# Seven of eight blocks of the second pass with seven products instead of five of eight

## The chip, the cores and the metric

The kernel runs on one core of a Trainium2 chip. The metric is the device time of one execution in microseconds (us), here the median of several. The core has TensorE (PE, with its weight loads as PEld), VectorE (DVE), ScalarE (ACT), GpSimd (POOL) and SyncE (SP), which here issues nearly all DMAs. Each engine works through its own queue in program order; engines wait for each other by semaphores. SBUF is the on-chip memory, PSUM the accumulators of TensorE.

## The reference

Lightning attention over 4 x 8 heads gives x (4 x 768 x 512). A mixer follows, and then a two-layer network whose hidden layer has 2048 columns. Everything is fp32; the weights arrive as 64-bit numbers.

```python
xt = x.transpose(0, 2, 1)
h = xt @ U @ V                                # rank 32 along the sequence
u = x + h.transpose(0, 2, 1)                  # 3072 rows of 512
ch = np.maximum(u @ w_ch1, 0.0) @ w_ch2       # 512 -> 2048 -> 512
return (u + ch).astype(np.float32)
```

`u @ w_ch1` is the first product, with its result r kept in DRAM until the second product, `max(r, 0) @ w_ch2`, reads it.

## The kernel before, in words

**fp32 by parts.** A product of fp32 numbers is made of three products of rounded parts. Each operand is split into a high part (ScalarE, a multiplication by nearly one), a low part (VectorE, the operand minus its high part) and a third (a combination of the two, on VectorE or POOL). One product over 128 input channels is then three matmuls of 128x512: high by high and low by low into one accumulator, third by third into another, or into the same one after `raise_high` (ScalarE, in place) has scaled it between. The matmuls of the first two parts are called highs below, those of the third part thirds. A `raise_high`, or a drain of PSUM by ScalarE (`taken`) or VectorE (`add_to`, L1190), stands between them.

**The first product** goes over 24 groups of 128 rows, four to a column group g of 512, so g = 0 to 5, and over 16 tiles ft of 128 columns of the hidden layer. Groups 0 to 3 are the first pass. From 144 us on it runs as 56 units, one (g, ft) each of 12 matmuls (`run_unit`, L989): the highs of this unit, then the thirds of the unit two before. In each unit, steps of other work are emitted that have been strewn over units by number (`strew`, L1041): converting the 64-bit words of a tile of w1 or w2 to fp32 (`weight_steps`, L114: a load of 512 KB of words, five VectorE and two ScalarE instructions), splitting it (w1) or keeping it in DRAM (w2), and preparing what the second pass needs. A step that comes at unit n is placed on its engine behind what was emitted before.

**The second pass** does groups g0 = 4 and g1 = 5 in eight blocks j, each of two column tiles ft = 2j and 2j + 1. Input channels are halved too, so a block is a 2 x 2 by 2 x 2 product of quarters: a11, a12 (u of g0, lower and upper channels), a21, a22 (g1) and the four quarters of the weights. A block in `eight_of` (L1262) makes the plain eight products, 48 matmuls. A block in `seven_of` (L1205) uses Winograd's form with seven products of sums and differences, 42 matmuls. The forms of u are a11, a12, s1 = a21 + a22, s2 = s1 - a11, s4 = a12 - s2, s3 = a11 - a21, a22, and a21 for plain blocks. Those of the weights are the four quarters and four differences, made by VectorE (`form_steps`, L1009, four instructions a block) and kept in DRAM (`forms_d`). The results of a seven are assembled from PSUM by VectorE's `add_to` and stored with `give`; an eight drains with ScalarE alone.

The order of products in a seven is (0, a11), (4, s1), the seventh product (7, a22) of the block before, (1, a12), (5, s2), (3, s4), (6, s3). `SEVEN` (L944) names the blocks with seven products: 0, 2, 3, 5 and 6. In the code z, d, p5, p3 and c11 are the accumulators of a seven; `pz` are those of a plain block.

**The stream.** The weight forms come back in the order of use (`sequence`), two to a tile, through `divided_steps` (L255): a load of two times 128 KB by SP into one of three wf buffers, a high on ScalarE (L276), a low on VectorE (L279) and a third on POOL (L285). Each product in the second pass calls `tick` once after its highs, which emits what is strewn at that step (or tick). Tile t, used from step 2t on, is loaded at step 2t - 8, gets its high at 2t - 4 and its low and third at 2t - 3 (L1151). Its splits go to a rotation of five tiles. Steps also hold the last four w2 conversions (`W2_LATE`, L946), the splits of the first four tiles of w2 (`w2_split`, L1361) and the first fetches and splits of r for the second product (`fetch`, `split`, into rm and m).

**The forms of u** (`form`, L1097) are made in the last ten units and the first steps: a high on ScalarE (L1103), a rest on VectorE (L1106, into s_hl) and a third on VectorE (L1109, into s_d), each over 128x1024. The list `late` holds ScalarE work that is emitted at the start of the next unit or step.

**The second product** goes over g and ft, four 128-row groups each, 1152 matmuls, with ScalarE and VectorE splitting r (L1303 to L1305) three steps ahead.

All orders named are written out by hand and kept on each engine; only behind the second pass a scheduler interleaves the first steps of the second product with the last of the pass.

Of the kernel before, what the change touches and what calls it, by code (L numbers as in the profile page):

```python
# [18 lines left out]
def kernel(  # L19
# [28 lines left out]
    nc = tc.nc  # L48
# [38 lines left out]
    late = []  # L87
# [167 lines left out]
    def divided_steps(parts, fetch, engine, apart=False, raw=None):  # L255

        st = {}

        def load():
            st["w"] = raw() if raw and apart else plain({}, 0)()  # L260
            fetch(st["w"])

        def split():
            hi, low, third = parts()
            w = st["w"][:, 0 : hi.shape[-1]]
            nc.scalar.mul(hi, w, E * NEAR)
            nc.vector.scalar_tensor_tensor(
                low, hi.bitcast(FP32), -1.0 / E, w, ALU.mult, ALU.add
            )
            engine.tensor_tensor(  # L270
                out=third, in0=low.bitcast(FP32), in1=hi.bitcast(FP32), op=ALU.subtract
            )

        def high():
            st["hi"], st["low"], st["third"] = parts()
            nc.scalar.mul(st["hi"], st["w"][:, 0 : st["hi"].shape[-1]], E * NEAR)  # L276

        def low():
            nc.vector.scalar_tensor_tensor(  # L279
                st["low"], st["hi"].bitcast(FP32), -1.0 / E,  # L280
                st["w"][:, 0 : st["hi"].shape[-1]], ALU.mult, ALU.add,
            )

        def third():
            engine.tensor_tensor(  # L285
                out=st["third"], in0=st["low"].bitcast(FP32), in1=st["hi"].bitcast(FP32),
                op=ALU.subtract,
            )

        return [load, high, low, third] if apart else [load, split]  # L290
# [562 lines left out]
    def enter_first_product(s):  # L853
        nonlocal r_pool
        att_ctx.close()
        words_pool[:] = [wconv]
        r_pool = ctx.enter_context(tc.tile_pool(name="r", bufs=8, reuse_waits="tile"))
        set_ends(r_pool.tile([P, P], FP32, tag="ends", bufs=1, name="ends"))
        more_w.append(ctx.enter_context(tc.tile_pool(name="w1_more", bufs=2, reuse_waits="tile")))
        plain_pool.append(  # L860
            ctx.enter_context(tc.tile_pool(name="plain", bufs=2, reuse_waits="tile"))
        )
        whole_pool.append(
            whole_ctx.enter_context(tc.tile_pool(name="whole", bufs=NG - FG, reuse_waits="tile"))
        )
# [62 lines left out]
    for i, (pair, ft) in enumerate(head):  # L928
# [8 lines left out]
    mix_ctx.close()  # L937
    sums_pool = whole_ctx.enter_context(tc.tile_pool(name="sums", bufs=2, reuse_waits="tile"))
    tags.append(("wt", "wf"))
    words_pool += 2 * [  # L940
        mid_ctx.enter_context(tc.tile_pool(name="words", bufs=2, side="right", reuse_waits="tile"))
    ]
    HC = C // 2
    SEVEN = (0, 2, 3, 5, 6)  # L944
    LAST = FT - 4
    W2_LATE = (6, 8, 24, 26)  # L946


    one = iter(range(1 << 30))
# [91 lines left out]
    def strew(units, steps):  # L1041
        assert len(units) == len(steps)
        for n, step in zip(units, steps):
            at.setdefault(n, []).append((units[0], step))
# [9 lines left out]
    strew((4, 4, 5, 5, 5), form_steps(0))  # L1054
    for ft, n in ((4, 3), (5, 7)):
        strew(after(n, FIRST), w1_steps(ft))
    for ft, n in zip(range(6, FT), (10, 14, 18, 22, 26, 28, 32, 33, 35, 37)):
        strew(after(n, W1), w1_steps(ft))
    for n in (5, 9, 12, 16, 20, 24, 30, 39, 42, 45, 48, 51):
        strew(after(n, W2), later.pop(0))  # L1060
    for j, n in ((2, 9), (3, 16), (4, 25), (5, 30), (6, 35), (7, 40)):
        strew((n, n, n + 1, n + 1, n + 1) if j in SEVEN else (n,), form_steps(j))
    units = [(g, ft) for ft in range(2, LAST) for g in range(FG)]
    units += [(g, ft) for g in range(FG) for ft in range(LAST, FT)]
# [12 lines left out]
    for n in range(0, len(sequence), 2):  # L1077

        def parts(n=n):
            stream[n // 2] = t = w_tile(FT + n // 2)  # L1080
            k = HC * len(sequence[n : n + 2])
            return [t[:, i, 0:k] for i in range(3)]

        def fetch(w, n=n):
            for i, (j, form) in enumerate(sequence[n : n + 2]):
                nc.sync.dma_start(out=w[:, i * HC : (i + 1) * HC], in_=forms_d[j][:, form])

        stream_steps.append(divided_steps(parts, fetch, nc.gpsimd, True))

    places, form_of = {}, {}  # L1090

# [5 lines left out]
    def form(key, n, i, of):  # L1097

        hl, d = form_of[key] = places[n][i]
        hi, low = hl[:, 0], hl[:, 1]  # L1100

        def high():
            nc.scalar.mul(hi, of, NEAR)  # L1103

        def rest():
            nc.vector.tensor_tensor(out=low, in0=of, in1=hi.bitcast(FP32), op=ALU.subtract)  # L1106

        def last():
            nc.vector.scalar_tensor_tensor(  # L1109
                d, hi.bitcast(FP32), E, low.bitcast(FP32), ALU.mult, ALU.subtract  # L1110
            )

        return [high, rest, last]
# [16 lines left out]
    for n, (g, ft) in enumerate(units):  # L1130
        if n == 46:
            place(0)
            strew((46, 47, 48), form("a11", 0, 0, a11))
            strew((47, 48, 49), form("a12", 0, 1, a12))
            strew((50,), sums(a12, a12, s2))
        if n == 50:
            place(1)
            strew((50, 51, 52), form("s1", 1, 0, s1))
            strew((51, 52, 53), form("s2", 1, 1, s2))
            strew((53,), sums(s3, a11, a21))  # L1140
        if n == 54:
            place(2)
            strew((54, 55, 55), form("s4", 2, 0, a12))
            a22_steps = form("a22", 2, 1, a22)
            strew((55,), a22_steps[:1])
        run_unit(g, ft, sorted(at.pop(n, ()), key=lambda what: what[0]))
    assert not at
    strew((0, 0), stream_steps[2][2:])
    strew((1, 2, 2), stream_steps[3][1:])
    for t in range(4, len(stream_steps)):  # L1150
        strew((2 * t - 8, 2 * t - 4, 2 * t - 3, 2 * t - 3), stream_steps[t])  # L1151
    strew((0, 0), a22_steps[1:])
    def last_forms():
        place(3)
        s3_steps, a21_steps = form("s3", 3, 0, s3), form("a21", 3, 1, a21)
        strew((1, 2, 2), s3_steps)
        strew((3, 4, 4), a21_steps)
        strew((4,), [forms_made])

    def forms_made():  # L1160
        whole_ctx.close()
# [199 lines left out]
    def w2_split(ft):  # L1361
        def raw():
            t = e_pool[0].tile([P, 3, C], F32R, tag="e", name="w2")
            w2t[ft] = [t[:, i, :] for i in range(3)]
            return w2t[ft][2].bitcast(FP32)

        if ft >= 4 and ft % 4 == 0:
            hl = hl_pool.tile([P, 4, 2, C], F32R, tag="hl", name="w2_hl")
            d = d_pool.tile([P, 4, C], F32R, tag="d", name="w2_d")
            for i in range(4):  # L1370
                w2t[ft + i] = [hl[:, i, 0], hl[:, i, 1], d[:, i]]
        return divided_steps(
            lambda: w2t[ft], lambda w: nc.sync.dma_start(out=w, in_=w2_d[ft]), nc.vector,
            ft < 4, raw,
        )

# [9 lines left out]
    strew((total - 14,), [begin_second])  # L1386
    for ft in range(4):
        strew(
            (total - 13 + 2 * ft, total - 6 + ft, total - 5 + ft, total - 5 + ft), w2_split(ft)
        )  # L1390
    for n in range(3):
        strew((total - 5 + n,), [lambda n=n: fetch(n)])
# [64 lines left out]
```

## Time and profile before

| what | us |
|---|---|
| median of 3 runs | 649.53 (649.27 to 653.06) |
| the profiled execution | 649.79 |
| its span, first to last instruction | 648.0 |
| TensorE busy, share of the span | 636.8, 98% |
| VectorE busy | 449.9, 69% |
| ScalarE busy | 329.7, 51% |
| POOL busy | 141.3, 22% |
| first pass in units (PE) | 142 to 295 |
| second pass in blocks (PE) | 295 to 382 |
| second product (PE) | 382 to 644 |

Most busy times in the profile are of pipelined instructions: a 128x512 matmul is listed with 389 ns, and the next one starts long before it ends. What counts is the distance of starts. In a timeline row stand the start, the time that the row's instructions cover, the engine, the line, the operation, output and inputs, and how many instructions were merged; in brackets the idle time before them and what ended it. DVE rows of 0.68 us that follow each other start 0.60 apart. The granted clock is the share of full speed that TensorE was allowed.

### The profile page before, as it was taken

The numbers are of one execution on the slowest core, as the hardware profiler recorded it, in microseconds if no ns is written. First come the engines' busy times: TensorE is split into PE (matmuls) and PEld (weight loads), VectorE is DVE, ScalarE is ACT, GpSimd is POOL, SyncE is SP. The second block draws the span as 40 slices with busy tenths as digits, with TensorE's granted clock in tenths as the row PEclk, the third lists the DMA queues.
The fourth block names the chain that finished last, engine by engine and source line by source line (L and its number), as shares of the span: only waits on it lengthen the run. The fifth ranks groups of instructions, "written<-read, shape, count | busy, mean of one in ns | idle before, by whom it ended". The sixth has DMA issues, their size and how long they took to land.

```text
span 648.0 us, 13566 instructions
## 1 busy us (share of the span) xinstructions
PE 636.8 (98%) x5212; PEld 534.0 (82%) x5212; DVE 449.9 (69%) x714; ACT 329.7 (51%) x604; POOL 141.3 (22%) x120
## 2 busy tenths in 40 slices
PE   8999999999999999999999999999999999999997
PEld 7989989778888888886878878888888888888886
DVE  5766878567776688589867799785575665755754
ACT  3775766436676777678657574232322322322320
POOL 3575978000000000013343400030030300300300
PEclk9999999999999999999999999999999999999999
DMA  9979985348967787456577798353362353442521
GB/s 227 249 181 277 246 224 159 128 165 295 312 238 272 248 281 258 180 204 228 196 232 240 252 301 281 103 190 134 96 228 98 121 204 99 170 155 97 180 82 65
DMA packets 140227, 127.91 MB, mean 197 GB/s; under 512 B 82370, under 2 KB 97602, under 8 KB 140162
## 3 DMA queue, kind: packets, MB, share of 16 engines
q1 hardware_dynamic: 115040, 120.62, 58.0%
q10 hardware_dynamic: 25122, 6.42, 4.4%
q8 instruction: 41, 0.67, 0.4%
q14 instruction: 24, 0.20, 0.1%
HBM read 77.86 MB, written 48.76 MB: 195 GB/s over the span
## 4 chain that ended last, share of the span: by engine, by line
PE 74%; DVE 1%; issue 1%; DMA 1%; ACT 0%; DVEq 0%; SPq 0%; ACTq 0%
PE pz L957 28%; PE pz L1321 13%; PE pz L1319 13%; PE pd L1323 13%; PE z L957 2%; PE p L957 1%; DMA wf<-forms_d 1%; PE d L957 1%; DVE s_hl L1106 1%; PE c L957 1%; PE pd L900 0%; DVE w L279 0%; PE pz L889 0%; ACT p L964 0%; ACT s_hl L1103 0%
## 5 line engine op out<-in xcount | busy, mean ns | idle before, releaser
L1303 ACT ACTIVATE m<-rm 128x512 fp32r<-128x512 f32 x96 | 60.6, 631 | 168.3 <-PE pd L1323 141.3
L1304 DVE SCALAR_TENSOR_TENSOR m<-rm,m 128x512 fp32r<-128x512 f32 x96 | 71.6, 746 | 84.1 <-ACT m L1303 84.1
L1319 PE MATMUL pz<-w_hl,m 128*128 128x512 f32 x288 | 112.0, 389 | 0.0
L1321 PE MATMUL pz<-w_hl,m 128*128 128x512 f32 x288 | 112.0, 389 | 0.0
L1323 PE MATMUL pd<-w_d,m 128*128 128x512 f32 x288 | 110.7, 389 | 0.0
L957 PE MATMUL pz<-u_hl,w 128*128 128x512 f32 x448 | 110.3, 389 | 0.0
L957 PEld LDWEIGHTS pz<-u_hl,w 128*128 128x128 f32 x448 | 84.1, 188 | 17.4
L285 POOL TENSOR_TENSOR w<-w 128x512 fp32r<-128x512 f32 (+1 forms) x24 | 35.1, 1468 | 227.9 <-DVE w L279 208.3
L1305 DVE SCALAR_TENSOR_TENSOR m<-m 128x512 fp32r<-128x512 f32 x96 | 74.4, 776 | 2.7
L1348 POOL TENSOR_TENSOR o<-o,u 128x512 f32<-128x512 f32 x20 | 29.8, 1518 | 198.5 <-DVE o L1344 198.5
L1319 PEld LDWEIGHTS pz<-w_hl,m 128*128 128x128 f32 x288 | 54.1, 188 | 11.3
L1321 PEld LDWEIGHTS pz<-w_hl,m 128*128 128x128 f32 x288 | 54.1, 188 | 11.2
L1323 PEld LDWEIGHTS pd<-w_d,m 128*128 128x128 f32 x288 | 54.1, 188 | 11.2
L957 PE MATMUL pz<-u_d,w 128*128 128x512 f32 x224 | 59.7, 389 | 0.0
L964 ACT ACTIVATE pz<-pz 128x512 f32<-128x512 f32 x68 | 39.4, 581 | 31.8 <-PE pz L957 31.8
L957 PEld LDWEIGHTS pz<-u_d,w 128*128 128x128 f32 x224 | 42.0, 188 | 8.8
L196 DVE SCALAR_TENSOR_TENSOR sc<-words,sc 128x512 uint32<-128x512 uint32 (+2 forms) x34 | 24.5, 721 | 34.8 <-ACT sc L178 34.8
L968 ACT ACTIVATE r<-pz 128x512 f32<-128x512 f32 x68 | 40.2, 594 | 14.2 <-PE pz L957 13.2
L472 DVE TENSOR_TENSOR sm<-pss,mask 128x512 f32<-128x512 f32 x48 | 30.9, 685 | 19.3 <-PE pss L463 19.3
L1319 PE MATMUL pz<-w,m 128*128 128x512 f32 x96 | 37.4, 390 | 0.0
L1321 PE MATMUL pz<-w,m 128*128 128x512 f32 x96 | 37.4, 389 | 0.0
L1323 PE MATMUL pd<-w,m 128*128 128x512 f32 x96 | 37.3, 390 | 0.0
(143 smaller groups left out, 1081.4 us busy)
## 6 DMA issues: line engine op xcount, KB each, us to landing
r_d<-r SPq DMA_DIRECT2D x96, 256.0 KB, 2.4
rm<-r_d SPq DMA_DIRECT2D x96, 256.0 KB, 2.6
words<-in_moe_w_ch_dram SPq DMA_DIRECT2D x30, 512.0 KB, 4.5
u_d<-x_nat SPq DMA_DIRECT2D x24, 256.0 KB, 4.1
u<-u_d SPq DMA_DIRECT2D x24, 256.0 KB, 4.3
wf<-forms_d SPq DMA_DIRECT2D x47, 128.0 KB, 3.1
qraw<-in_q_dram SPq DMA_DIRECT2D x23, 256.0 KB, 5.1
out_dram<-o SPq DMA_DIRECT2D x23, 256.0 KB, 2.0
```

Source lines behind the costliest of these rows:

```text
L285: engine.tensor_tensor(out=st["third"], in0=st["low"].bitcast(FP32), in1=st["hi"].bitcast(FP32), op=ALU.subtract,)
L472: nc.vector.tensor_tensor(out=sm[:, x], in0=pss[:, x], in1=mask[:, x], op=ALU.mult)
L957: nc.tensor.matmul(out=out, lhsT=weights, rhs=moving, start=start and i == 0, stop=i == len(pieces) - 1, skip_group_check=not start,)
L964: nc.scalar.mul(acc, acc, 1.0 + E)
L968: nc.scalar.mul(r, acc, 4096.0)
L1303: nc.scalar.activation(out=m[:, 0], in_=r, func=AF.Relu, scale=NEAR)
L1304: nc.vector.scalar_tensor_tensor(m[:, 1], r, 0.0, hi, ALU.max, ALU.subtract)
L1305: nc.vector.scalar_tensor_tensor(m[:, 2], hi, E, low, ALU.mult, ALU.subtract)
L1319: nc.tensor.matmul(out=pz, lhsT=m[:, 0, cols], rhs=hi, start=first, stop=False)
L1321: nc.tensor.matmul(out=pz, lhsT=m[:, 1, cols], rhs=low, start=False, stop=end)
L1323: nc.tensor.matmul(out=pd, lhsT=m[:, 2, cols], rhs=third, start=first, stop=end)
L1348: nc.gpsimd.tensor_tensor(out=o, in0=o, in1=u, op=ALU.add)
```

## The change

Blocks 4 and 7 become sevens: `SEVEN` is now 0 and 2 to 7, and only block 1 makes eight products. The stream then has 53 forms in 27 tiles instead of 47 in 24. The rest moves or re-places other work:

- Of u's forms, s4 and s3 are made before the second pass, with their high parts first on ScalarE at unit 54; a22 and a21 are made in its first eight steps. Before, s4 and a22 came first and s3 and a21 in the steps.
- The thirds of the stream's first four tiles are made by VectorE, not POOL; the thirds of w2's first four tiles by POOL, not VectorE.
- Conversions of w1 and w2 in the units come at other units, the last of w2 starting at 46 instead of 51; the four late ones start at steps 7, 9, 16 and 22 instead of 6, 8, 24 and 26.
- The first four w2 splits are spread from 24 to 3 steps ahead of the pass's end instead of 13 to 2.
- The pool of words gets three buffers instead of two (four places with the first one), the pool of r seven instead of eight.

```diff
-        r_pool = ctx.enter_context(tc.tile_pool(name="r", bufs=8, reuse_waits="tile"))
+        r_pool = ctx.enter_context(tc.tile_pool(name="r", bufs=7, reuse_waits="tile"))
...
-    words_pool += 2 * [
-        mid_ctx.enter_context(tc.tile_pool(name="words", bufs=2, side="right", reuse_waits="tile"))
+    words_pool += 3 * [
+        mid_ctx.enter_context(tc.tile_pool(name="words", bufs=3, side="right", reuse_waits="tile"))
     ]
     HC = C // 2
-    SEVEN = (0, 2, 3, 5, 6)
+    SEVEN = (0, 2, 3, 4, 5, 6, 7)
     LAST = FT - 4
-    W2_LATE = (6, 8, 24, 26)
+    W2_LATE = (7, 9, 16, 22)
...
-    for ft, n in zip(range(6, FT), (10, 14, 18, 22, 26, 28, 32, 33, 35, 37)):
+    for ft, n in zip(range(6, FT), (10, 11, 15, 17, 20, 25, 29, 30, 32, 36)):
         strew(after(n, W1), w1_steps(ft))
-    for n in (5, 9, 12, 16, 20, 24, 30, 39, 42, 45, 48, 51):
+    for n in (6, 16, 21, 24, 27, 34, 38, 40, 42, 43, 45, 46):
         strew(after(n, W2), later.pop(0))
-    for j, n in ((2, 9), (3, 16), (4, 25), (5, 30), (6, 35), (7, 40)):
+    for j, n in ((2, 9), (3, 13), (4, 19), (5, 27), (6, 32), (7, 38)):
         strew((n, n, n + 1, n + 1, n + 1) if j in SEVEN else (n,), form_steps(j))
...
-        stream_steps.append(divided_steps(parts, fetch, nc.gpsimd, True))
+        stream_steps.append(
+            divided_steps(parts, fetch, nc.vector if n < 8 else nc.gpsimd, True)
+        )
...
             place(2)
-            strew((54, 55, 55), form("s4", 2, 0, a12))
-            a22_steps = form("a22", 2, 1, a22)
-            strew((55,), a22_steps[:1])
+            s4_steps, s3_steps = form("s4", 2, 0, a12), form("s3", 2, 1, s3)
+            late.extend([s4_steps[0], s3_steps[0]])
+            strew((54, 54), s4_steps[1:])
+            strew((55, 55), s3_steps[1:])
...
-    strew((0, 0), a22_steps[1:])
     def last_forms():
         place(3)
-        s3_steps, a21_steps = form("s3", 3, 0, s3), form("a21", 3, 1, a21)
-        strew((1, 2, 2), s3_steps)
-        strew((3, 4, 4), a21_steps)
-        strew((4,), [forms_made])
+        strew((1, 3, 4), form("a22", 3, 0, a22))
+        strew((5, 6, 8), form("a21", 3, 1, a21))
+        strew((8,), [forms_made])
...
-            lambda: w2t[ft], lambda w: nc.sync.dma_start(out=w, in_=w2_d[ft]), nc.vector,
+            lambda: w2t[ft], lambda w: nc.sync.dma_start(out=w, in_=w2_d[ft]),
+            nc.gpsimd if ft < 4 else nc.vector,
             ft < 4, raw,
...
-            (total - 13 + 2 * ft, total - 6 + ft, total - 5 + ft, total - 5 + ft), w2_split(ft)
+            (total - 24 + 5 * ft, total - 20 + 5 * ft, total - 19 + 5 * ft, total - 18 + 5 * ft),
+            w2_split(ft),
```

## The prediction

> **What bounds the kernel now.** I read the page's table of busy time first, then the groups, then the windows of the seven-product stage, and last the chain and the timeline around each gap.
>
> ```profile
> PE 636.8 (98%) x5212; PEld 534.0 (82%) x5212; DVE 449.9 (69%) x714; ACT 329.7 (51%) x604; POOL 141.3 (22%) x120
> ...
> 144.40 147.80 PE pz L957 x652
> ```
>
> TensorE is the bound, and the second line (the chain in order of time) gives its price: 652 matmuls of 128x512 in 147.80 us, 0.2267 us each, with no gap from 144 to 292 us. From 384 us to the end the second product keeps the same pace. So the change can win in two ways only: fewer matmuls, and fewer gaps between 292 and 384 us, the second pass with blocks. The windows show where these gaps are.
>
> ```profile
> 290.00:300.00 10.00, 10.00 (x45) 8.09 (x44) 8.76 (x7) 8.07 (x15) 4.16 (x3) 1.00 0.63 211
> 300.00:310.00 10.00, 8.39 (x30) 6.17 (x29) 9.86 (x11) 5.47 (x9) 2.82 (x3) 0.83 0.57 193
> ...
> 330.00:340.00 10.00, 9.70 (x43) 7.74 (x42) 7.26 (x12) 6.02 (x11) 5.37 (x4) 1.00 0.84 264
> 370.00:380.00 10.00, 9.65 (x43) 7.66 (x42) 9.05 (x15) 6.60 (x14) 1.19 (x2) 1.00 0.88 304
> 390.00:400.00 10.00, 10.00 (x46) 8.29 (x45) 9.15 (x16) 3.58 (x6) 0.00 (x0) 1.00 0.90 306
> ```
>
> The columns are busy PE, PEld, DVE, ACT and POOL, then granted clock, DMA share and GB/s. A full slice has 45 or 46 matmuls; 300:310 has 30, and its clock is 0.83. I count the matmuls between two starts on PE's timeline, times 0.2267, against the time between them. Start, 294.74 (first block's `z`) to 320.21 (third block's `z`): 94 matmuls, 21.3 us of work in 25.47, **4.2 lost**. Blocks 2 and 3, to 339.39: 82 matmuls, 18.6 in 19.18, **0.6 lost**. Blocks 4 to 6, to 369.33: nothing. End, to 384.21 in the second product: **1.3 lost**. Together 6.1 us.
>
> The start, on the timelines of PE, DVE and POOL:
>
> ```profile
> 302.00 2.21 POOL L285 TENSOR_TENSOR w<-w 128x512 fp32r<-128x512 f32 x1 [1.76 <-DVE w L279]
> 303.16 2.12 DVE L1109 SCALAR_TENSOR_TENSOR s_d<-s_hl 128x1024 fp32r<-128x1024 f32 x1
> 305.21 0.68 DVE L1190 SCALAR_TENSOR_TENSOR r<-d,r 128x512 f32<-128x512 f32 x1
> 306.03 1.02 PE L957 MATMUL d<-s_d,w 128*128 128x512 f32 x2 [1.57 <-DVE r L1190]
> 307.69 2.91 PE L957 MATMUL pz<-s_hl,w 128*128 128x512 f32 x8
> ```
>
> VectorE is never idle from 294 to 312: forms of u (128x1024), lows of the stream (L279) and drains (L1190) stand in one queue, and PE waits for a drain that stands behind a form. The pause costs twice: windows of 2 us have a granted clock of 0.56 and 0.59 at 306:310, and eight matmuls take 2.7 us instead of 1.8. The shorter pause at 338.5 leaves the clock at 1.00.
>
> **Part by part.** *Blocks 4 and 7 with seven products.* A product here is 6 matmuls; 8 become 7 in two blocks: 12 x 0.2267 = **-2.7 us** on the path itself.
>
> *Start.* The drains that PE waits for come behind less. Two whole conversions of w2 (L170 to L201, 2 x 0.33 + 3 x 0.60 = 2.5 us each) leave the units just before the stage; s4 and s3 are formed before it, a22 and a21 after; and four POOL thirds become DVE work (L285 on DVE at 374.00: 0.68 each, 0.60 from start to start where they follow each other). By rows a 128x1024 form takes 1.22 alone and 2.1 to 2.3 beside a POOL third, so four thirds for 2.4 us of DVE take away four slowings of about 1 us. [...]
>
> I went through VectorE's new order with the durations of before. ScalarE forms s4 and s3 at 290.0 to 292.3; VectorE ends their rests and thirds at about 297, the stream's third and fourth tiles at 298 and 301, a22's low at 302.2, and the drain that was late at 302.9, ahead of PE's `d` at 303.85. What is late next is a21: its low part comes behind four drains, at about 308.8, and PE wants it at 308.2. I cost that at 0.6 plus 0.2 of start-up, **0.8 lost** instead of 4.2. Bounds: 0 (VectorE 0.6 earlier) and 2.7 (0.8 with the 1.8 us that the lower clock cost at 306:310). The copy of s4's and s3's high parts ahead of `raise_high` on ScalarE delays that by 1.9 us; it is wanted 3.6 us after, so it costs nothing.
>
> *The run of blocks 2 to 7.* All six are sevens now; before, never more than two in a row. A seven has 42 matmuls, 9.52 us, and asks of VectorE 7 drains and 3.5 lows at 0.60, 6.3 us, of ScalarE some 5.9, of POOL 3.5 x 1.3 = 4.5. That fits, but the last two late w2 conversions now start at steps 16 and 22, inside this run, instead of 24 and 26, in and just behind an eight: for four steps (5.4 us) VectorE has 3.6 + 2.5 = 6.1. And the loads are close:
>
> ```profile
> 332.57 0.81 SPq L1086 DMA_DIRECT2D wf<-forms_d  x2
> ...
> 337.65 0.63 ACT L276 ACTIVATE w<-wf 128x512 fp32r<-128x512 f32 x1 [2.12 <-DMA wf<-forms_d]
> 338.19 0.58 ACT L964 ACTIVATE p<-p 128x512 f32<-128x512 f32 x1
> ...
> 338.83 0.73 PE L957 MATMUL p<-s_d,w 128*128 128x512 f32 x2 [0.30 <-ACT p L964]
> ```
>
> ScalarE works in order: a high (L276) that waits for its load holds the `raise_high` behind it, and PE waits for that. Block 3 lost 0.6 so, block 6 nothing (its ScalarE waited 0.8). Blocks 3 to 7 are now all second-in-a-row blocks: five times the mean 0.3 is 1.5; the two conversions at 0.4 to 1.3 add about 0.7. I take **2.2 lost** instead of 0.6; bounds 0 and 7 (five times 1.0, the cost of the loop below, and 2). w2's first four splits now lie inside the run, one per five steps, 0.5 ScalarE, 0.60 DVE, 1.3 POOL: cover for all three is there (3 us spare on each), at most 0.6 if a step is full, within that bound.
>
> *The end.* Block 7 is a seven. VectorE is relieved of eight w2 instructions (374 to 381, 4.8 us) and given seven drains (4.2) in a block 1.4 us shorter. Between the last c12 drain and the drain that PE's last `d` waits for stand now two w2 splits and the first m, nine instructions, 5.4 us, against 20 matmuls, 4.5: 0.9 lost; the second m's third comes 0.5 late; 0.6 for restarts. **2.0 lost** instead of 1.3; bounds 0.5 and 4 (rm's load is asked for three steps, 4.1 us, ahead, and landed in 4.6).
>
> *Elsewhere.* Eight more form differences (L1020, about 0.4 each) and 1 MB of stores in 144 to 292 us, where VectorE has 102 us of work in 140 by the windows, and each w1 tile is ready one or more units ahead, the margin it had before: 0, and about 1 us if a words load were late by more than a unit. Six more loads of forms of 128 KB are in the run's sum. One r buffer less: a seven hands out four, so the seventh back is over a block (9.5 us) old, and stores land in 2.6: 0. The fourth place for words takes waits off SP: 0.
>
> **Sum.** -2.7, -3.4 (start), +1.6 (run), +0.7 (end): -3.8 on the profiled execution's 649.79, which is 0.26 above the median: **646.0 us**, lost time 5.0 instead of 6.1.
>
> **Rivals.** *All gaps close* (0.20): VectorE's relief carries through the run and the end: lost 0.5, 649.8 - 2.7 - 5.6 = 641.5; block 6, without loss at 279 GB/s, speaks for it, the fuller VectorE at the end against it; 641.5 to 643.5. *The stream cannot keep up with sevens in a row, and it is slower* (0.15). A tile of two forms is wanted each 2.72 us; with three wf buffers a round may take 8.16. It takes 5.1 from issue to high (332.57 to 337.65), 0.6 high, 0.6 low, which leaves 1.9 for the low to wait in VectorE's queue. Three drains in a row are 2.07 (329.83), a w2 conversion 2.5: past 1.9 each round holds PE. At 1 us per block for five, 2 for the two conversions, one drop of the clock (1.8) and 2.7 for start and end, 11.5 are lost: 649.8 - 2.7 - 6.1 + 11.5 = 652.5. It decides the sign from 1.2 us per block on. For it: block 3; against: blocks 5 and 6. *The new order doesn't do what it says* (0.10): PE still loses 4.2 at the start because ScalarE's s3 waits for its sum: 649.4. [...]
>
> My forecast has 0.55, 644 to 649. Range 641.8 to 652.8: the lowest sum of all bounds is 641.5, the highest 654.7, and both at once leave out under 2 in 10. A change within 1% (6.5 us) is about what a measurement can't tell from none: faster by more (below 643.0) 0.17, most of the first rival; slower by more (over 656) 0.06; within, 0.77.
>
> **What would show it.** PE with 12 matmuls fewer; first `z` to third `z` about 22 us instead of 25.5, clock 1.00 throughout; the next gap at the eight's second accumulator behind s_hl L1106's successor; gaps under 0.6 in blocks 3 to 5 behind L276; 1 to 2 us before the second product. Wrong if ScalarE's L276 waits grow from block to block, or if a slice of the run shows a clock under 1.

## The result

| | before | after |
|---|---|---|
| median of 21 runs each, us | 649.39 (647.13 to 653.06) | 652.54 (650.20 to 656.17) |
| ratio after to before | | 1.0051 (95%: 1.0036 to 1.0066) |
| span of the profiled execution | 648.0 | 649.7 |
| matmuls on PE | 5212 | 5200 |
| first block's `z` starts at | 294.74 | 293.87 |

The change makes the kernel slower by 0.5%, some 3.3 us, where 3.5 less were forecast. Below are the line of busy time in the page's table for the kernel after and, under it, the row of its chain in order of time that answers to the 652 matmuls of before (start, time covered, operation and count):

```profile
PE 635.3 (98%) x5200; PEld 528.9 (81%) x5200; DVE 469.1 (72%) x739; ACT 331.7 (51%) x607; POOL 144.8 (22%) x123
```

```profile
143.53 145.08 PE pz L957 x640
```

The twelve matmuls are gone, and the pace of 0.2267 us is the same (145.08 / 640). VectorE has 25 instructions and 19.2 us more. What the matmuls gave was lost in gaps. The windows of the kernel after, with the columns as in the prediction (busy PE, PEld, DVE, ACT, POOL, granted clock, DMA share, GB/s):

```profile
290.00:300.00 10.00, 10.00 (x45) 8.06 (x44) 8.36 (x10) 8.16 (x15) 0.00 (x0) 1.00 0.59 199
300.00:310.00 10.00, 8.84 (x38) 6.72 (x37) 9.27 (x14) 5.78 (x11) 1.62 (x2) 1.00 0.74 249
...
330.00:340.00 10.00, 9.72 (x40) 7.00 (x39) 9.96 (x15) 6.11 (x12) 4.62 (x4) 1.00 0.78 253
340.00:350.00 10.00, 8.11 (x33) 5.75 (x33) 8.11 (x13) 5.74 (x11) 4.67 (x4) 1.00 0.64 210
...
360.00:370.00 10.00, 8.66 (x37) 6.47 (x37) 6.55 (x11) 6.12 (x12) 5.82 (x4) 1.00 0.57 190
...
380.00:390.00 10.00, 9.18 (x36) 6.06 (x36) 10.00 (x17) 5.51 (x9) 1.25 (x1) 1.00 0.83 275
```

The first holes, in 300:310, are smaller (38 matmuls instead of 30, clock 1.00 instead of 0.83). New ones stand in 340:350 (33 of 45) and 360:370 (37), where the kernel before lost nothing, and the end at 380:390 has 36.

To compare kernels I use one count throughout: from the first `z` of a block to that of the next, the time less the matmuls between them at 0.22669; for block 7, the 130 matmuls from its `z` on. Outside these stretches, from 150 us on, TensorE loses nothing in any of the kernels below (at most 0.03).

| lost, us | b0 | b1 | b2 | b3 | b4 | b5 | b6 | b7 and end | sum |
|---|---|---|---|---|---|---|---|---|---|
| before | 2.98 | 1.18 | 0.02 | 0.57 | 0.02 | 0 | 0 | 1.30 | 6.08 |
| after | 0.41 | 1.94 | 0 | 1.19 | 2.80 | 0 | 1.97 | 3.11 | 11.42 |

From the first `z` to the end of the span that makes -2.72 + 5.34 = +2.62 us; the two traces have 353.26 and 355.83 there, +2.57. The spans differ by 1.7 only, because the first `z` came 0.87 earlier. The stretch ahead of it differs from one execution to the next (293.70 to 298.52 in the profiles of this study), so the count after it is the steadier one. Even there, a stretch that an edit leaves alone differs from profile to profile: in the kernels below block 0 loses 0.16 to 1.00, block 6 1.27 to 1.97 and the end 3.08 to 3.95 where nothing is changed for them. Each count is from one profile, so a difference within these bounds shows nothing.

**Where the four gaps come from.** The start, on the timeline of the kernel after (ScalarE, VectorE and PE):

```profile
302.51 0.63 ACT L276 ACTIVATE w<-wf 128x512 fp32r<-128x512 f32 x1 [1.11 <-DMA wf<-forms_d]
...
305.12 0.69 DVE L1191 SCALAR_TENSOR_TENSOR r<-d,r 128x512 f32<-128x512 f32 x1 [0.62 <-ACT r L1195]
305.72 2.08 DVE L1191 SCALAR_TENSOR_TENSOR r<-p,r 128x512 f32<-128x512 f32 x3
307.72 1.22 DVE L1108 TENSOR_TENSOR s_hl<-u_whole,s_hl 128x1024 fp32r<-128x1024 f32 x1
308.99 1.89 PE L957 MATMUL pz<-s_hl,w 128*128 128x512 f32 x7 [1.16 <-DVE s_hl L1108]
```

PE waits for a21's low (307.72), as the prediction had it. That low stands behind four drains, and these are late because ScalarE held the drain's first half behind a high that waited 1.11 for its load, and behind a21's own high (303.56, 1.04 us).

Block 4, on the same view with SP:

```profile
331.29 1.67 DVE L201 SCALAR_TENSOR_TENSOR wg<-m,sc 128x512 f32<-128x512 f32 x1
...
336.08 1.19 DVE L170 TENSOR_SCALAR sc<-words 128x512 uint32<-128x512 uint32 x1
...
338.24 4.21 SPq L1199 DMA_DIRECT2D r_d<-r  x3
...
339.93 2.07 DVE L1191 SCALAR_TENSOR_TENSOR r<-p,r 128x512 f32<-128x512 f32 x3
341.92 0.68 DVE L196 SCALAR_TENSOR_TENSOR sc<-words,sc 128x512 uint32<-128x512 uint32 x1
342.63 0.69 DVE L201 SCALAR_TENSOR_TENSOR wg<-m,sc 128x512 f32<-128x512 f32 x1
343.24 0.69 DVE L279 SCALAR_TENSOR_TENSOR w<-w,wf 128x512 fp32r<-128x512 f32 x1
343.98 0.96 PE L957 MATMUL z<-s_hl,w 128*128 128x512 f32 x3 [1.19 <-DVE w L279]
...
346.15 0.63 ACT L276 ACTIVATE w<-wf 128x512 fp32r<-128x512 f32 x1 [2.98 <-DMA wf<-forms_d]
```

PE waits for the low of a stream tile (343.24) that stands behind three drains and two instructions of the late w2 conversion (L196, L201). VectorE has no pause from 325.60 to 345.90. Three rows of the two conversions start beside a POOL row and are long: 1.67 for L201 (the first line; POOL from 330.83 for 1.58 us) against 0.69 at 342.63, and 0.89 (325.60) and 1.19 (336.08) for L170 (POOL from 324.91 and 335.70, 1.29 each) against 0.42 at 205.14. Added up, the rows of the two take 4.3 and 3.7 us, against 2.9 at 202 to 210 us, where POOL does nothing. SP shows a second suspect: its three stores cover 338.24 to 342.45, as it waits for the same late drains, and the loads behind them are issued only then; ScalarE waits 2.98 for one.

Block 6:

```profile
358.25 4.51 SPq L1199 DMA_DIRECT2D r_d<-r  x3
...
360.35 2.07 DVE L1191 SCALAR_TENSOR_TENSOR r<-p,r 128x512 f32<-128x512 f32 x3
...
362.86 0.91 SPq L1086 DMA_DIRECT2D wf<-forms_d  x2
...
367.52 0.63 ACT L276 ACTIVATE w<-wf 128x512 fp32r<-128x512 f32 x1 [3.06 <-DMA wf<-forms_d]
368.69 1.19 PE L957 MATMUL z<-s_hl,w 128*128 128x512 f32 x4 [1.26 <-ACT r L1195]
```

Here no conversion is near. Loads of forms wait on SP behind the stores of c12 and c22; ScalarE's high waits 3.06 for such a load, the drain of `z` (L1195) stands behind the high, and PE behind the drain.

The end:

```profile
376.76 1.38 SPq L1298 DMA_DIRECT2D rm<-r_d  x3
...
380.37 0.63 ACT L1304 ACTIVATE m<-rm 128x512 fp32r<-128x512 f32 x1 [0.60 <-DMA rm<-r_d]
...
380.62 1.18 DVE L270 TENSOR_TENSOR w_d<-w_hl 128x512 fp32r<-128x512 f32 x1
381.73 0.68 DVE L267 SCALAR_TENSOR_TENSOR w_hl<-w_hl,wf 128x512 fp32r<-128x512 f32 x1
382.33 0.68 DVE L1305 SCALAR_TENSOR_TENSOR m<-rm,m 128x512 fp32r<-128x512 f32 x1
...
383.53 0.68 DVE L1306 SCALAR_TENSOR_TENSOR m<-m 128x512 fp32r<-128x512 f32 x1
...
383.06 0.73 PE L1322 MATMUL pz<-w,m 128*128 128x512 f32 x2 [0.32 <-DVE m L1305]
384.26 0.73 PE L1324 MATMUL pd<-w,m 128*128 128x512 f32 x2 [0.24 <-DVE m L1306]
```

rm is asked for at 376.76, and ScalarE's first m starts at 380.37, 0.60 late for its load. It is done at 381.00, though, and VectorE's queue comes to m's low (L1305) only at 382.33, behind a third and a low of w2's splits (L270, L267); m's third (L1306) stands behind another. Both pauses of PE shown end with these two rows, a third one at 386.66 with a drain on VectorE. VectorE has no pause from 368.7 to 390.

### The profile page after: what moved, and what is told of

Its sections match the earlier page's. It is cut to its first block, busy times and chain, and to the rows that moved or that the text cites. A ratio compares the mean times of both kernels' runs of the same rounds, so it can differ in the third digit from the quotient of the medians.

```text
span 649.7 us, 13595 instructions
## 1 busy us (share of the span) xinstructions
PE 635.3 (98%) x5200; PEld 528.9 (81%) x5200; DVE 469.1 (72%) x739; ACT 331.7 (51%) x607; POOL 144.8 (22%) x123
## 4 chain that ended last, share of the span: by engine, by line
PE 87%; DVE 5%; DMA 3%; ACT 2%; issue 2%; SPq 0%; POOL 0%; DVEq 0%; ACTq 0%; POOLq 0%
PE pz L957 23%; PE pz L1322 13%; PE pd L1324 13%; PE pz L1320 13%; PE pss L463 4%; PE px L514 4%; PE z L957 2%; PE pz L889 2%; PE px L525 2%; PE pqk L416 2%; PE p L957 2%; PE pkv L486 1%; DMA wf<-forms_d 1%; DVE r L1191 1%; PE d L957 1%
## 5 line engine op out<-in xcount | busy, mean ns | idle before, releaser
L1305 DVE SCALAR_TENSOR_TENSOR m<-rm,m 128x512 fp32r<-128x512 f32 x96 | 71.6, 746 | 81.6 <-ACT m L1304 81.5
L285 POOL TENSOR_TENSOR w<-w 128x512 fp32r<-128x512 f32 (+1 forms) x27 | 38.2, 1426 | 229.2 <-DVE w L279 221.8
L1306 DVE SCALAR_TENSOR_TENSOR m<-m 128x512 fp32r<-128x512 f32 x96 | 74.6, 778 | 2.6
L964 ACT ACTIVATE pz<-pz 128x512 f32<-128x512 f32 x60 | 34.8, 580 | 26.9 <-PE pz L957 26.8
L968 ACT ACTIVATE r<-pz 128x512 f32<-128x512 f32 x60 | 35.8, 596 | 15.3 <-PE pz L957 14.9
L196 DVE SCALAR_TENSOR_TENSOR sc<-words,sc 128x512 uint32<-128x512 uint32 (+2 forms) x34 | 24.6, 725 | 20.5 <-ACT sc L178 20.5
```

Source lines behind the costliest of these rows:

```text
L285: engine.tensor_tensor(out=st["third"], in0=st["low"].bitcast(FP32), in1=st["hi"].bitcast(FP32), op=ALU.subtract,)
L964: nc.scalar.mul(acc, acc, 1.0 + E)
L968: nc.scalar.mul(r, acc, 4096.0)
L1305: nc.vector.scalar_tensor_tensor(m[:, 1], r, 0.0, hi, ALU.max, ALU.subtract)
L1306: nc.vector.scalar_tensor_tensor(m[:, 2], hi, E, low, ALU.mult, ALU.subtract)
```

## The experiments

All are compared with the kernel before on the same chip. Two theories carry the first set. V: whole conversions of w2 in a run of sevens fill VectorE's queue. S: stores on SP, waiting for late drains, hold the loads behind them.

**The stores later.** On the kernel after; the stores of c12 and c22 are issued in the next block, ahead of its last product.

```diff
-        give(c12, f2, g0)
         add_to(c22, five)
-        give(c22, f2, g1)
         def end():
+            give(c12, f2, g0)
+            give(c22, f2, g1)
             on_chain(7, "a22")
```

> The changed kernel, with the stores of c12 and c22 of a seven put on SP's queue behind the first two steps of the next block, so that no load of a weight form stands behind them. Nothing is left out. In the profile of the changed kernel blocks 4 and 6, whose first form has an even number in the stream (24 and 38), lost 2.8 and 2.0 us, and in both ScalarE's high waited 3 us for a load that SP had issued right behind these stores. Theory S (the loads stand behind the stores on SP): block 6 loses under 0.4, block 4 under 1.5, and the time is 2.5 to 4 us under the changed kernel's, about that of the kernel before. Rival V (VectorE is too full in the run of sevens): blocks 3, 4 and 6 lose what they lost, and the time is within 1 us of the changed kernel's.

652.77 us, ratio 1.0030 (1.0011 to 1.0049). Block 6 falls from 1.97 to 0.23, block 4 stays at 2.79, the end is at 3.70. The time falls by less than S said. In block 4 the high that waited 2.98 for its load now waits for none, and PE pauses as before:

```profile
347.34 0.62 ACT L276 ACTIVATE w<-wf 128x512 fp32r<-128x512 f32 x1
...
348.23 0.96 PE L957 MATMUL z<-s_hl,w 128*128 128x512 f32 x3 [1.20 <-DVE w L279]
```

So block 6 is S, and block 4 isn't: in the kernel after its load was late too, and cost PE nothing.

**Without two conversions.** On the kernel after, those at steps 16 and 22 are left out, and the last two tiles of w2 are read from the place of the one before them.

```diff
-    W2_LATE = (7, 9, 16, 22)
+    W2_LATE = (7, 9)
...
-            lambda: w2t[ft], lambda w: nc.sync.dma_start(out=w, in_=w2_d[ft]),
+            lambda: w2t[ft], lambda w: nc.sync.dma_start(out=w, in_=w2_d[min(ft, FT - 3)]),
...
-    assert not later
+    later.clear()
```

> The changed kernel without the two late w2 conversions at steps 16 and 22; the last two tiles of w2 are read from the place of the one before, so two conversions are left out. Rival V (VectorE full, its two conversions in front of lows and drains): blocks 3 and 4 lose under 0.5 instead of 1.2 and 2.8, block 6 what it lost, and the time is 3 to 4 us shorter. Theory S: block 3 loses under 0.5, block 4 still 1.5 to 2.5, as block 6 its 2.0, and the time is 1.5 to 2.5 us shorter.

649.96 us, ratio 0.9984 (0.9967 to 1.0001). Block 3 falls from 1.19 to 0, block 4 from 2.80 to 0.45, block 6 keeps 1.44. Blocks 3 and 4 are V: SP's long store there was a consequence of the late drains.

**Seven products alone.** On the kernel before, nothing else changed.

```diff
-    SEVEN = (0, 2, 3, 5, 6)
+    SEVEN = (0, 2, 3, 4, 5, 6, 7)
```

> The kernel before with blocks 4 and 7 as sevens and nothing else of the change. Theory S: blocks 4 and 6 begin at even numbers here too and lose about 2 each, the start keeps its 4.2, the end loses over 3, and with 2.7 fewer for 12 matmuls the time is 2 to 5 us over the kernel before. Rival V: blocks 4 and 5 lose for the conversions at steps 24 and 26, block 6 nothing. Had the forecast been right on sevens in a row, the time would be within 1 us of the kernel before or under it.

655.21 us, ratio 1.0063 (1.0040 to 1.0087). Blocks 0 and 1 lose 4.17, as before (4.16). Block 4, where the conversions at steps 24 and 26 now fall into a run of sevens, loses 3.89 (0.02), block 6 0.18 (0), the end 5.26 (1.30). The two further sevens without the rest of the change therefore lose 7.5 us for 2.7 saved. Block 6 loses almost nothing here, where the first w2 splits come late as in the kernel before, which suggests that stores ahead of loads hurt only beside the splits that the change puts into the run.

**The sevens undone.** On the kernel after; the rest of the change stays.

```diff
-    SEVEN = (0, 2, 3, 4, 5, 6, 7)
+    SEVEN = (0, 2, 3, 5, 6)
...
-        strew((n, n, n + 1, n + 1, n + 1) if j in SEVEN else (n,), form_steps(j))
+        strew((n, n, n + 1, n + 1, n + 1) if j in SEVEN else (n + 1,), form_steps(j))
```

> The changed kernel with plain blocks 4 and 7 again, all else as changed (the forms of a plain block are kept one unit later, so that its splits are done). All sevens of the run begin at odd numbers. Theory S: blocks 2, 3, 5 and 6 lose together under 1.5 (block 3 its 1.2 or less), start 2.4 as in the changed kernel instead of 4.2, end 1 to 2: 1 to 3 us under the kernel before. Rival V: block 3 loses its 1.2 and block 4, with the second conversion, 1 or more.

651.49 us, ratio 1.0012 (0.9990 to 1.0033). Blocks 0 and 1 lose 1.98 instead of 4.16: the rest of the change, u's new order of forms among it, gains 2.2. Block 3 loses 1.14 and block 4 1.01 although block 4 is plain, and the end loses 3.12 with a plain block 7. So the end loses 1.8 more by the rest of the change too, of which the re-placed w2 splits stand nearest; by the run before, the further sevens alone do the same and more.

**Conversions back in the units.** On the kernel after; those of steps 16 and 22 go to units 13 and 48, and nothing is left out.

```diff
-    W2_LATE = (7, 9, 16, 22)
+    W2_LATE = (7, 9)
...
-    for n in (6, 16, 21, 24, 27, 34, 38, 40, 42, 43, 45, 46):
+    for n in (6, 13, 16, 21, 24, 27, 34, 38, 40, 42, 43, 45, 46, 48):
```

> Edit: the two conversions of w2 that stand at steps 16 and 22 of the run of sevens go back into the 144 to 292 us stretch (at units 13 and 48), so nothing is left out; all else as in the changed kernel. Theory V (VectorE's queue holds the run of sevens wherever a whole conversion, 2.5 to 3.6 us beside POOL, falls into it): block 3 loses 0 to 0.3 instead of 1.19, block 4 loses 0.3 to 0.6 instead of 2.80 (as where the two conversions were left out), the stretch before stays without loss because VectorE is busy there 3.7 to 4.5 us of 6 at these places; the time falls by some 3.3 us against the changed kernel, to 649.3, ratio to the kernel before 0.999 to 1.001. Rival (the work costs the same wherever it stands): the loss turns up before the first block, as a start of the first z over 1 us later, or in block 0 by the same amount, and the ratio stays at 1.004 to 1.006.

649.46 us, ratio 1.0005 (0.9985 to 1.0025); block 3 loses 0, block 4 0.37, blocks 0 and 1 2.01, the units nothing. V holds with its numbers. A conversion moves whole, though, with its two ScalarE instructions and its load of 512 KB, so VectorE's part is not priced by itself; for it speak the queue without a pause and the rows that PE waited for. Windows of this kernel, with the same columns:

```profile
330.00:340.00 10.00, 10.00 (x46) 8.29 (x45) 7.05 (x11) 7.01 (x13) 6.35 (x5) 1.00 0.59 200
340.00:350.00 10.00, 9.93 (x44) 7.92 (x43) 6.95 (x11) 6.41 (x13) 3.99 (x4) 1.00 0.72 243
```

VectorE has 7.05 and 6.95 of 10 instead of 9.96 and 8.11, and PE is full.

**a21 a step earlier.** On the kernel after.

```diff
-        strew((5, 6, 8), form("a21", 3, 1, a21))
+        strew((4, 5, 7), form("a21", 3, 1, a21))
```

> Edit: a21's high, low and third are formed at steps 4, 5 and 7 instead of 5, 6 and 8; all else as in the changed kernel. Theory Q (block 1's second accumulator waits for a21's low because that form stands behind three drains of p, 2.1 us, on VectorE): with the form ahead of them the wait of 1.16 at 309 goes, block 1 loses 0.3 to 0.8 instead of 1.94 and the time falls by 1.1 to 1.6. Rival F (VectorE is simply full there, 5.9 of 6 us in 306 to 312): the drains behind the form are late instead, PE waits for one of them, and blocks 0 and 1 together lose 2.0 to 2.6 as now (2.35).

651.91 us, ratio 1.0033 (1.0015 to 1.0050). Block 1 falls from 1.94 to 0.01, but block 0 rises from 0.41 to 1.21; together 1.22 instead of 2.35. On the timeline of this kernel:

```profile
303.60 0.63 ACT L276 ACTIVATE w<-wf 128x512 fp32r<-128x512 f32 x1 [0.97 <-DMA wf<-forms_d]
304.14 1.04 ACT L1105 ACTIVATE s_hl<-u_whole 128x1024 fp32r<-128x1024 f32 x1
...
305.72 0.73 PE L957 MATMUL p<-s_d,w 128*128 128x512 f32 x2 [0.77 <-ACT p L964]
```

Q gets its wait, and the loss that comes instead is not F's drain on VectorE: the form's high (L1105, 1.04) now stands ahead of `raise_high` on ScalarE, behind a high that waits for its load.

**More thirds on POOL.** On the kernel after, those of w2's tiles 4 to 7.

```diff
-            nc.gpsimd if ft < 4 else nc.vector,
+            nc.gpsimd if ft < 8 else nc.vector,
```

> Edit: the thirds of w2's tiles 4 to 7 are formed on POOL, as those of tiles 0 to 3 are, instead of VectorE; all else as in the changed kernel. Theory D (the end is held by VectorE's queue, busy without a gap from 370 to 392): four instructions of 0.60 to 1.2 us leave the queue in 380 to 392, the end loses 1.0 to 1.8 instead of 3.11 and the time falls by 1.3 to 2. Rival L (the end is held by loads, of rm and of w2's tiles, that hold ScalarE): the end still loses 2.8 to 3.4. Rival B (the POOL thirds slow the VectorE instructions beside them from 0.60 to about 1.2, which eats the gain): VectorE's m rows take over 1 us and the end loses 3 or more.

653.58 us, ratio 1.0062 (1.0039 to 1.0085); the end loses 4.74 instead of 3.11. D's gain doesn't appear. On its timeline:

```profile
380.62 0.63 ACT L266 ACTIVATE w_hl<-wf 128x512 fp32r<-128x512 f32 x1 [2.52 <-DMA wf<-w_d]
...
384.58 1.65 DVE L1306 SCALAR_TENSOR_TENSOR m<-m 128x512 fp32r<-128x512 f32 x1
...
386.29 0.50 PE L1324 MATMUL pd<-w,m 128*128 128x512 f32 x1 [1.14 <-DVE m L1306]
```

ScalarE waits 2.52 for a load of w2 (0.18 in the kernel after), and m's third takes 1.65 beside a POOL row (384.02, 1.66 us) instead of 0.68, which is B and holds PE for 1.14. But that load was asked for at 375.57, ahead of the first instruction that this edit moves (382.12), so its lateness is not the edit's doing, and at the second product's first matmul (383.23) PE had lost 1.7 more than in the kernel after, behind ScalarE. This run therefore doesn't decide against VectorE's queue.

**rm earlier.** On the kernel after.

```diff
-        strew((total - 5 + n,), [lambda n=n: fetch(n)])
+        strew((total - 9 + n,), [lambda n=n: fetch(n)])
```

> Edit: the first three loads of the second product's rows (rm) are asked for four steps, some 5.4 us, earlier; all else as in the changed kernel. Theory L (the bound named in the prediction: rm is asked for 4.1 us ahead and lands in 4.6, so ScalarE's m waits 0.60 at 380.4 and the last drains stand behind it): that wait goes, the end loses 1.7 to 2.5 instead of 3.11. Theory D (VectorE's queue is what ends last at the end): the end still loses 2.8 to 3.4, since m's two VectorE parts stand behind the same drains.

651.68 us, ratio 1.0042 (1.0021 to 1.0063). The end loses 1.65 instead of 3.11, just below L's range. On its timeline:

```profile
380.54 0.62 ACT L1304 ACTIVATE m<-rm 128x512 fp32r<-128x512 f32 x1
...
384.17 0.70 PE L957 MATMUL d<-s_d,w 128*128 128x512 f32 x2 [0.23 <-DVE r L1191]
```

ScalarE's m waits for no load, and PE's last `d` follows at 384.17. The scheduler also moved the w2 splits that stood ahead of m's low on VectorE behind the drains (the first low now starts at 388.74), and those are what PE's pauses in the kernel after stood behind. This run doesn't divide the 1.46 between the load and the order. Block 4 lost 4.41 here with nothing changed there, 1.6 more than in the kernel after; the last section shows the slower clock behind it.

**Three moves together.** On the kernel after: the conversions in the units, rm earlier, and a21 with its high one step further ahead, in ScalarE's wait for the load.

```diff
-        strew((5, 6, 8), form("a21", 3, 1, a21))
+        strew((3, 5, 7), form("a21", 3, 1, a21))
```

> Edit: three moves together on the changed kernel: the two conversions of w2 in the units 13 and 48 instead of steps 16 and 22; rm's first three loads four steps earlier; a21's high, low and third at steps 3, 5 and 7 (the high one step ahead of the variant before, into the 0.97 us in which ScalarE waited there for a load of forms). Nothing is left out. Theory V with L (each of these moves acts in its own stage and the gains add): blocks 0 and 1 lose 0.3 to 0.9 instead of 2.35, block 3 nothing, block 4 0.2 to 0.5, block 6 1.3 to 2.0 as in the changed kernel, the end 1.5 to 2.2; 3.7 to 5.5 in all instead of 11.42. Against the kernel before (6.08 lost, twelve matmuls more) that is -3.3 to -5.1, ratio 0.992 to 0.995. Rival M (a gap that is taken away lets VectorE and the loads arrive at the next place as late as before, so the sum stays): 7 or more are lost, ratio 0.999 or above.

647.27 us, ratio 0.9954 (0.9931 to 0.9977). Lost: 0.51 and 0.85 in blocks 0 and 1, 0.14 in 2, 0 in 3, 0.22 in 4, 0 in 5, 1.84 in 6, 1.64 at the end, 5.19 in all. That is inside the bounds of V with L for the sum, though the start lost 1.36 where 0.3 to 0.9 were expected; M falls.

**Four moves.** The same with the stores later as in the first experiment.

> Edit: the three moves, and the stores of c12 and c22 given to SP in the next block ahead of its last product, so that no load of forms stands behind them. Nothing is left out. Theory S (block 6's 1.97 is SP's wait for the drains in front of the loads): block 6 loses 0 to 0.4, the rest as with the three moves, 2.3 to 4.0 in all, ratio to the kernel before 0.990 to 0.993. Rival E (the later stores only move the wait to the end, where the variant with this edit alone lost 3.70 instead of 3.11): block 6 as S has it, but the end loses 2.2 to 3 and the sum is that of the three moves, ratio 0.992 to 0.995.

643.47 us, ratio **0.9893 (0.9866 to 0.9920)**. Lost: 0.51, 0.85, 0.19, 0, 0, 0, 0.62, 1.03, in all 3.19. From the first `z` on it takes 347.6 us, 5.6 less than the kernel before. S is right with a little more left in block 6 than it had, and E's move of the wait to the end doesn't appear beside the earlier rm. Its windows:

```profile
300.00:310.00 10.00, 9.45 (x41) 7.19 (x40) 9.07 (x14) 5.55 (x11) 2.42 (x2) 1.00 0.74 246
...
340.00:350.00 10.00, 10.00 (x46) 8.29 (x45) 7.37 (x12) 7.43 (x14) 4.56 (x4) 1.00 0.52 171
360.00:370.00 10.00, 10.00 (x44) 7.98 (x44) 8.50 (x14) 6.84 (x15) 8.64 (x6) 1.00 0.79 256
370.00:380.00 10.00, 9.43 (x41) 7.30 (x40) 8.77 (x14) 6.62 (x12) 3.00 (x3) 1.00 0.96 321
```

340:350 is full where the kernel after had 33 matmuls; small holes remain at the start and the end.

**What the two further sevens are worth then.** The kernel with four moves, with blocks 4 and 7 plain again.

```diff
-    SEVEN = (0, 2, 3, 4, 5, 6, 7)
+    SEVEN = (0, 2, 3, 5, 6)
...
-        strew((n, n, n + 1, n + 1, n + 1) if j in SEVEN else (n,), form_steps(j))
+        strew((n, n, n + 1, n + 1, n + 1) if j in SEVEN else (n + 1,), form_steps(j))
```

> Edit: the kernel with the four moves, but blocks 4 and 7 with eight products as in the kernel before (twelve matmuls more, their weights stored without the four differences). Theory P (the two further sevens are worth their twelve matmuls, 2.72, once nothing else is in the way, since blocks 4 to 6 lose nothing in the kernel with the four moves): the loss stays 2.5 to 4.0, the time is 1.9 to 3.5 above the kernel with the four moves, some 646.2, ratio to the kernel before 0.992 to 0.996. Rival W (an eight gives VectorE and the loads slack that the block after it lives on): the loss falls to 0.5 to 1.5, the time is within 1 us of the kernel with the four moves, ratio 0.988 to 0.991.

647.92 us, ratio 0.9980 (0.9962 to 0.9998). It loses 3.72, and from the first `z` on takes 350.9 us, 3.3 more than with four moves: the twelve matmuls and 0.5. By the trace that is P. The ratio is above P's 0.992 to 0.996, and lies further from that of four moves (0.0087, 5.6 us) than the traces do; the two were measured on different chips, and the stretch ahead of the first `z` varies by more than what is left between ratio and traces.

**The four moves without rm's.**

```diff
-        strew((total - 9 + n,), [lambda n=n: fetch(n)])
+        strew((total - 5 + n,), [lambda n=n: fetch(n)])
```

> Edit: the kernel with the four moves, with rm's first three loads at the changed kernel's steps again. Theory L (at the end it is rm's load that holds ScalarE, and the drains and m's parts behind it): the end loses 2.5 to 3.7 instead of 1.03, the time is 1.5 to 2.7 above the kernel with the four moves, ratio to the kernel before 0.991 to 0.995. Rival D (VectorE's queue alone, which the other moves relieved too, since block 6 no longer comes late): the end loses 1.0 to 1.6, ratio 0.989 to 0.990.

645.72 us, ratio 0.9951 (0.9935 to 0.9967). The end loses 2.55 instead of 1.03, the other blocks the same to 0.02. On its timeline:

```profile
376.37 1.27 ACT L266 ACTIVATE w_hl<-wf 128x512 fp32r<-128x512 f32 x2 [1.00 <-DMA wf<-w_d]
...
377.04 1.33 DVE L267 SCALAR_TENSOR_TENSOR w_hl<-w_hl,wf 128x512 fp32r<-128x512 f32 x1 [0.47 <-ACT w_hl L266]
378.47 0.69 DVE L270 TENSOR_TENSOR w_d<-w_hl 128x512 fp32r<-128x512 f32 x1
379.08 0.68 DVE L1191 SCALAR_TENSOR_TENSOR r<-c,r 128x512 f32<-128x512 f32 x1
...
379.91 0.47 PE L1320 MATMUL pz<-w,m 128*128 128x512 f32 x1 [1.00 <-ACT m L1304]
```

L's size holds, but its path is another. The load that ScalarE waits 1.00 for is w2's; the low and third of that tile come late on VectorE and stand ahead of a drain (379.08). PE goes on 0.15 after that drain's end, while the first m's high, to which the row puts the wait down, was done at 378.91 (start 378.28). With rm asked for earlier, the scheduler puts that drain and m ahead of w2's splits (the drain at 372.24 in the kernel with four moves). So at the end the order of w2's splits, m and drains in VectorE's queue and the landing of w2's load act together, and no run here separates them.

## Why the prediction was wrong

**Twelve matmuls, -2.72.** Right: 5200 against 5212, at the same pace. With the gaps mended, 3.3 us lie between seven and five sevens from the first `z` on.

**Start, -3.4.** The mechanism was right and the size was off. The gap stands where the prediction put it, at block 1's second accumulator behind a21's low, at clock 1.00. That low ended at 308.9, where 308.8 was worked out. But PE wanted it at 307.7 and not 308.2, and block 0's 0.41 and 0.4 for the third at 313.79 come on top: 2.35 lost instead of 0.8, inside the bounds of 0 to 2.7. The gain was 1.8.

**Run of blocks 2 to 7, +1.6.** This is the step that failed. 2.2 lost were expected, and blocks 2 to 6 lost 5.96 (block 7 is counted with the end). One term was too small and another had the wrong mechanism (3.6 + 0.37 and 1.97 make the 5.96).
- "The two conversions at 0.4 to 1.3 add about 0.7": they cost 3.6 (1.19 + 2.80, against 0 + 0.37 with them in the units). VectorE's excess of 0.7 us in four steps (6.1 in 5.4) was in the working, but with a conversion at 2.5, as it runs alone. Beside POOL the rows of the two took 4.3 and 3.7 instead of 2.9, VectorE had no pause for 20 us, and the low that PE wanted stood behind three drains and two rows of the conversion. Whether the conversions would have fitted without POOL beside them was not tried. Late stores and a late load (2.98) were there in block 4 too, but didn't cost PE anything: without them it lost as much (2.79).
- "Second-in-a-row blocks at 0.3": there is no such toll. Blocks 2 and 5 lose nothing, block 6 loses 1.97, by stores ahead of loads; the order of `give` on SP was never priced. Late drains held the stores on SP (4.51 us for three, from 358.25), the loads of forms were issued behind those (362.86), and ScalarE, in order, held the next drain behind its wait for a load (3.06). "Cover is there" for the w2 splits failed at block 6 as well: with the splits late, 0.18; with the stores later, 0.23. The two together cost it, and no run divides them further.

**End, +0.7.** The path was right in the main and the size was off: 3.11 lost instead of 2.0, inside 0.5 to 4. VectorE's queue, on which the 2.0 rested, is what the pauses in the second product's first matmuls end with in the kernel after (383.06, 384.26, 386.66). With rm asked for earlier it is 1.65, and with the other moves 1.03; but that edit also changes the order of VectorE's queue, so the bound named, rm landing in 4.6 when asked for 4.1 ahead, isn't shown to have decided. How much each gives stays open.

**Elsewhere, 0.** Right: the units lose nothing, before and after. That the r buffer less costs nothing was not tried by itself; no wait for one was among the four gaps.

**The rivals.** The second had 11.5 lost, 652.5 us, and its sign-deciding 1.2 us per block: measured are 11.42 and a mean of 1.19 over blocks 2 to 6. That the sums agree is luck: it had 8.8 for the run and 2.7 for start and end, and 5.96 and 5.46 were lost. Its mechanism held only in part. The stream was late, but not by a toll on each round of three wf buffers: two of the five blocks (2 and 5) lose nothing, and the loss goes away with the same three buffers when two conversions and two stores are moved. "All gaps close" (0.5 lost) is what four moves come nearest to, at 3.19. The third was wrong: the start did change.

## What to carry to other kernels

Work that is placed by counting steps moves when the steps get shorter. Replacing an eight (50 matmuls in five steps, 2.3 us a step) by a seven (42 in seven, 1.36) brought every load, conversion and store that far nearer to what needs it, so before a product is taken out, count the lead of each in microseconds. When an engine's work is added up against the time it has, take its instructions at what they cost beside their neighbours (here 4.3 and 3.7 us for conversions that take 2.9 alone), and look at what stands in its queue ahead of the one that TensorE wants. Then follow the lateness through the queue that issues the loads: in block 6 stores that waited there made a load late (3.06), and the load the drain behind it on ScalarE. In block 4 such a late load (2.98) cost nothing, which only the run without it could tell. And test such moves together, since here none alone was faster than the kernel before and four were, by 1.1%.

## What the hardware showed unasked

**The same pause, two clocks.** Block 4 of the kernel with only rm earlier has the instructions and pauses of the kernel after: the longest is 1.20 us there and 1.19 here, with 1.9 us of PE idle in 340:346 in both. In the kernel after the clock stays at 1.00 (2.00 busy with ten matmuls in each of 346:348 and 348:350), in the kernel with rm earlier, by its windows:

```profile
344.00:346.00 2.00, 1.22 (x4) 0.73 (x5) 2.00 (x3) 0.00 (x0) 1.28 (x1) 1.00 0.67 207
346.00:348.00 2.00, 2.00 (x6) 1.56 (x6) 0.53 (x2) 1.12 (x2) 1.29 (x1) 0.55 0.86 288
348.00:350.00 2.00, 2.00 (x7) 1.52 (x7) 1.06 (x3) 1.21 (x2) 0.82 (x1) 0.59 0.83 266
```

Six and seven matmuls fit into 2 us there, and the block loses 1.6 us more (4.41 against 2.80). What decides between the two outcomes of the same pause, no run here shows. Of the profiles here, the kernel before alone had a slow clock at the start of the blocks, behind a pause of 1.57 us (306.03). The variant with sevens alone has the same order there, as little of 304:306 busy (0.44 of 2 us, 0.46 before) and 1.00 behind it, and lost as much (4.17 against 4.16), so the 1.8 us that the prediction gave to the slow clock isn't shown to have been lost by it.

**The front varies by itself.** Ahead of the units the kernels are alike, and the units lose nothing, but profiles differ by up to 4.8 us at the first `z`; in two of them (stores later, first `z` at 297.59; four moves without rm's, 298.52) the window 24:36 has a clock of 0.86. A difference of 1% between medians needs many runs for that reason; the count of lost time from the first `z` on is free of this part.

**A load's time to land.** Two loads of w2's tiles issued at 375.22 in the kernel after let ScalarE start at 377.91; issued at 375.57 in the variant with thirds on POOL, at 380.62: 2.7 and 5.1 us from the issue to the start behind it, for the same 256 KB each. A lead of 4 us would have covered the first and not the second.
